# Rebuilding the backward pass of sliding-window attention: batching heads, folding a row sum into a matmul, and transposing by DMA

## The chip, the cores and the metric

The kernel runs on one core of one Trainium2 chip. The metric is the time of one execution on the device, in microseconds (us). "Span" is the time from the first to the last instruction in a profiled execution. The engines are PE (matmul), PEld (its weight loads), DVE (vector), ACT (activation), POOL (GpSimd) and SP (which only issues DMA here).

## The reference

Four layers run in the order A, B, A, B, and the kernel returns the output and the gradients of the inputs. A is linear attention, B is attention over a window of 256 keys. T = 2048 tokens, D = 640, 32 heads of 20 columns. The change concerns the backward pass of B.

```python
def _B_ref(x, wqkv, wo):
    H = 32; Dh = D // H; W = 256
    q, k, v = ...                                   # of x @ wqkv, per head
    scores = jnp.einsum("bhqd,bhkd->bhqk", q, k) * (Dh ** -0.5)
    mask = (idx[:, None] - idx[None, :] >= 0) & (idx[:, None] - idx[None, :] < W)
    p = _softmax(jnp.where(mask, scores, -1e9))
    o = jnp.einsum("bhqk,bhkd->bhqd", p, v)
    return o... @ wo
# x = x + A(ln(x)); x = x + B(ln(x)); x = x + A(ln(x)); x = x + B(ln(x)); then jax.vjp
```

With dP = dO Vᵀ and delta = the row sum of dO·o, the gradient of the scores is dS = p · (dP − delta). Then dV = pᵀ dO, dK = dSᵀ Q and dQ = dS K.

## The kernel before

Heads are padded to 32 columns, so that four heads make a group of 128 columns; there are 8 groups. Queries come in 16 blocks of 128; a block sees at most three key blocks, 384 keys. So a layer B has 128 units (group, block). The kernel keeps both P and dS with queries on the partitions. As they lie, they are the stationary operand of the matmuls of dV and dK; for dQ it is dS transposed (the run no_transpose, which gives dQ dS as it lies, has wrong numbers: relative error 0.137).

```python
for g in range(G):
    QTg, KTg, VTg, dOTg, qsl, ksl, dosl, osl = ...   # slabs of this group, loaded on the queues of SP and ACT
    dtmp, delta = ...                                # DVE: row sums of dO * o, for the group
    for b in range(TT):
        ...                                          # four score matmuls into s4
        for hh in range(4):
            nc.scalar.activation(p_sb[:, 0:cw], s4[:, hh, 0:cw], ACT.Exp, bias=nll[...], scale=self.c_att)
            self.apply_masks(p_sb, nkt)              # two affine_select of 128 columns on POOL
        for hh in range(4):
            nc.tensor.matmul(dp_ps[:, 0:cw], lhsT=dOTg[...], rhs=VTg[...], ...)
            nc.vector.scalar_tensor_tensor(out=ds_sb[:, 0:cw], in0=dp_ps[:, 0:cw], scalar=delta[:, b, hh:hh + 1],
                                           in1=p_sb[:, 0:cw], op0=ALU.subtract, op1=ALU.mult)
            self.transposes(dsT_ps, [ds_sb[:, i * P:(i + 1) * P] for i in range(nkt)])    # on PE
            nc.scalar.copy(dsT[:, 0:nkt, :], dsT_ps[:, 0:nkt, :])                         # ACT
            for i in range(nkt):
                nc.tensor.matmul(dqvk[:, hh, 2, 0:DH], lhsT=dsT[:, i, :], rhs=ksl[...], ...)   # dq
        ...                                          # dv and dk of block b-2, copies to dqkv
```

Each unit is written head by head, in order; p is normalised by a bias in the exponential (minus the log of the row sum).

The softmax here doesn't subtract the row's maximum and nothing guards it: scores larger than these inputs give would overflow.

## Time and profile before

The median before was 4579.31 us (three runs, 4574.68 to 4580.05). The two backward attention stages, from their first score matmul to the last copy into dqkv, take 714 and 712 us, together 31% of the span.

| stretch of the profile before | us |
|---|---|
| backward attention of layer 3 (1794.5 to 2508.3) | 713.8 |
| backward attention of layer 1 (3211.5 to 3923.9) | 712.4 |
| the dO projection ahead of each | 52.8 and 52.6 |
| whole span | 4575.2 |

These lines are from the profile page of the kernel before: the span, the busy time of each engine, and two of the rows by slices (each digit is one fortieth of the span, about 114 us, in tenths).

```profile
span 4575.2 us, 81842 instructions
...
PE 3399.5 (74%) x31053; PEld 1892.7 (41%) x31148; DVE 2278.5 (50%) x6268; ACT 1870.0 (41%) x3758; POOL 577.0 (13%) x1963
...
PEclk6969655696865568555555996799555555798688
DMA  7345411334541136112110124214421120123312
```

Slices 17 to 22 and 29 to 34 lie in the backward attention stages: the clock granted to PE is 0.5 there, and the DMA engines are mostly at a fifth of their time or less.

The table of windows shows the first of those stages: the length, then busy microseconds of each engine with the number of instructions, the granted clock, the DMA share and the bytes per microsecond (GB/s).

```profile
core 0: us, PE busy (x) PEld busy (x) DVE busy (x) ACT busy (x) POOL busy (x), PEclk, DMA share, GB/s
1794.00:2508.00 714.00, 607.18 (x6784) 293.58 (x6784) 344.59 (x656) 506.30 (x1280) 264.44 (x960) 0.50 0.18 45
```

No engine is full. PE has 607 of 714 us, but that includes 12 transposes a unit, and the DMA engines have 0.18.

The costliest groups of instructions of the page, within the changed stages: line, engine, operation, tiles, shapes and count; then busy us in all and mean ns of one; then idle time of the engine just before them and what ended it.

```profile
L827 DVE SCALAR_TENSOR_TENSOR ds_sb<-dp_ps,delta,p_sb 128x384 bf16<-128x384 f32 (+2 forms) x1024 | 582.4, 590 | 555.7 <-POOL p_sb L474 472.6
L834 ACT COPY dsT<-dsT_ps 128x384 bf16<-128x384 bf16 (+2 forms) x1024 | 472.6, 462 | 346.7 <-PE dsT_ps L155 310.4
L814 ACT ACTIVATE p_sb<-s_ps,nll 128x384 bf16<-128x384 f32 (+2 forms) x1024 | 557.7, 573 | 12.4 <-issue 6.8
L155 PE MATMUL dsT_ps<-ident,ds_sb 128*128 128x128 bf16 x2880 | 499.7, 295 | 51.5 <-ACT dsT L834 40.5
L471 POOL TENSOR_SCALAR_AFFINE_SELECT p_sb<-p_sb 128x128 bf16<-128x128 bf16 x1024 | 308.6, 303 | 1583.5 <-ACT p_sb L814 1532.8
```

The view of waits, over 2060 to 2400 us of the kernel before, says who waited for whom, in all, how often, and the longest:

```profile
POOL p_sb L471 <- ACT p_sb L814: 200.8, 174, 3.2
DVE ds_sb L827 <- POOL p_sb L474: 126.9, 110, 2.2
PEld L836 <- ACT dsT L834: 93.7, 132, 0.9
ACT dsT L834 <- PE dsT_ps L155: 76.8, 121, 2.8
```

There is no single culprit: masks wait for the exponential, dS for the mask, the copy of the transposes for PE, and dQ for the copy. It is one ring of short waits (at most 3.2 us).

### The profile page before, as it was taken

Reading aid. Unit: us, or ns where it says so; the run is one execution under the profiler, and the core shown is the slowest. Engines: PE = TensorE matmul, PEld = TensorE weight load, DVE = VectorE, ACT = ScalarE, POOL = GpSimd, SP = SyncE. Lnnn points to the kernel's source line nnn. Section 1 sums busy time; section 2 is a strip of 40 time slices with the busy share of each in tenths; the row PEclk is TensorE's granted clock in tenths of the full one; section 3 lists DMA queues with packets and bytes.
Section 4 is the critical chain, followed back from the end, with each engine's and each line's share of the span. In section 5 each row is a group of like instructions: output and inputs, shape, how many; then the busy total and the mean of one; then the engine's idle time right before and its main releaser. Section 6 shows DMA issues by size and latency. Waiting matters only on the chain. (4 is left out here: it accounts for less than half of the span.)

```text
span 4575.2 us, 81842 instructions
## 1 busy us (share of the span) xinstructions
PE 3399.5 (74%) x31053; PEld 1892.7 (41%) x31148; DVE 2278.5 (50%) x6268; ACT 1870.0 (41%) x3758; POOL 577.0 (13%) x1963
## 2 busy tenths in 40 slices
PE   3759666675866666888888884688688888876577
PEld 2334333433433343444443453355344444354335
DVE  4764455566435542445444365444444544265436
ACT  1413445341335523777776120113677777220202
POOL 2000000000000000333333000000333333000000
PEclk6969655696865568555555996799555555798688
DMA  7345411334541136112110124214421120123312
GB/s 280 126 162 178 127 43 29 122 128 149 171 137 29 43 104 157 37 37 72 34 34 24 67 78 157 74 62 119 107 48 37 50 52 2 61 77 123 138 62 73
DMA packets 507340, 412.69 MB, mean 90 GB/s; under 512 B 329024, under 2 KB 479040, under 8 KB 505024
## 3 DMA queue, kind: packets, MB, share of 16 engines
q1 hardware_dynamic: 242976, 201.95, 14.5%
q10 hardware_dynamic: 263968, 205.49, 14.5%
q8 instruction: 245, 4.01, 0.4%
q14 instruction: 151, 1.24, 0.1%
HBM read 232.72 MB, written 174.65 MB: 89 GB/s over the span
## 5 line engine op out<-in xcount | busy, mean ns | idle before, releaser
L827 DVE SCALAR_TENSOR_TENSOR ds_sb<-dp_ps,delta,p_sb 128x384 bf16<-128x384 f32 (+2 forms) x1024 | 582.4, 590 | 555.7 <-POOL p_sb L474 472.6
L834 ACT COPY dsT<-dsT_ps 128x384 bf16<-128x384 bf16 (+2 forms) x1024 | 472.6, 462 | 346.7 <-PE dsT_ps L155 310.4
L814 ACT ACTIVATE p_sb<-s_ps,nll 128x384 bf16<-128x384 f32 (+2 forms) x1024 | 557.7, 573 | 12.4 <-issue 6.8
L155 PE MATMUL dsT_ps<-ident,ds_sb 128*128 128x128 bf16 x2880 | 499.7, 295 | 51.5 <-ACT dsT L834 40.5
L471 POOL TENSOR_SCALAR_AFFINE_SELECT p_sb<-p_sb 128x128 bf16<-128x128 bf16 x1024 | 308.6, 303 | 1583.5 <-ACT p_sb L814 1532.8
L823 PE MATMUL dp_ps<-VTg,dOTg 32*128 32x384 bf16 (+2 forms) x1024 | 439.5, 470 | 24.6 <-DVE ds_sb L827 19.5
L433 PE MATMUL sT_ps<-QTg,KTg 32*128 32x128 bf16 x2880 | 254.4, 296 | 160.4 <-DVE o_t L448 116.8
L836 PEld LDWEIGHTS <-dsT 128*128 128x128 bf16 x2880 | 156.0, 108 | 461.5 <-ACT dsT L834 393.3
L836 PE MATMUL dqvk_ps<-ksl,dsT 128*128 128x20 bf16 x2880 | 214.1, 183 | 117.8 <-ACT dsT L834 111.3
L474 POOL TENSOR_SCALAR_AFFINE_SELECT p_sb<-p_sb 128x128 bf16<-128x128 bf16 x896 | 266.9, 298 | 0.0
L807 PE MATMUL s_ps<-KTg,QTg 32*128 32x384 bf16 (+2 forms) x1024 | 240.6, 477 | 33.5 <-ACT p_sb L814 13.2
L155 PEld LDWEIGHTS <-ds_sb 128*128 128x128 bf16 x2880 | 227.4, 116 | 80.3 <-issue 68.4
L547 PEld LDWEIGHTS <-dqT 128*128 128x128 bf16 x1920 | 185.5, 99 | 132.8 <-DVE dqT L541 31.8
L543 ACT COPY dqT<-dqT_ps 128x896 bf16<-128x896 bf16 x64 | 58.0, 906 | 398.4 <-PE dqT_ps L155 391.6
L396 PE MATMUL qkvp_ps<-WBpad,hnT 128*128 128x512 bf16 x928 | 217.1, 384 | 3.6 <-ACT hnT L239 1.6
L515 PEld LDWEIGHTS <-hn_bw 128*128 128x128 bf16 x1280 | 126.9, 99 | 199.6 <-issue 74.0
L855 PEld LDWEIGHTS <-p_sb 128*128 128x128 bf16 x2880 | 156.7, 106 | 78.5 <-issue 76.2
L433 PEld LDWEIGHTS <-KTg 32*128 32x128 bf16 x2880 | 101.5, 112 | 197.2 <-DVE o_t L448 141.9
L287 PE MATMUL qkv_ps<-WA,hnT 128*128 128x512 bf16 (+1 forms) x626 | 148.5, 373 | 46.1 <-ACT vv L295 17.5
L855 PE MATMUL dqvk_ps<-dosl,p_sb 128*128 128x20 bf16 x2880 | 179.4, 181 | 3.3 <-ACT dqkv L863 2.7
L855 PE MATMUL dqvk_ps<-qsl,ds_sb 128*128 128x20 bf16 x2880 | 173.4, 179 | 0.0
L547 PE MATMUL dh_ps<-WqTB,dqT 128*128 128x320 bf16 x960 | 138.6, 304 | 25.5 <-DVE dqT L541 11.1
(2490 smaller groups left out, 5872.5 us busy)
## 6 DMA issues: line engine op xcount, KB each, us to landing
qkvp_126<-qkvp_slab SPq DMA_DIRECT2D x16, 768.0 KB, 3.5
qkvp_130<-qkvp_slab ACTq DMA_DIRECT2D x16, 768.0 KB, 3.4
qkvT_127<-qkvT_slab ACTq DMA_DIRECT2D x32, 256.0 KB, 5.2
qkvT_131<-qkvT_slab SPq DMA_DIRECT2D x32, 256.0 KB, 4.1
KTg<-qkvT_127 SPq DMA_DIRECT2D x12, 512.0 KB, 3.6
QTg<-qkvT_127 ACTq DMA_DIRECT2D x12, 512.0 KB, 4.8
QTg<-qkvT_131 ACTq DMA_DIRECT2D x12, 512.0 KB, 4.9
KTg<-qkvT_131 SPq DMA_DIRECT2D x12, 512.0 KB, 3.6
```

Of the source, the lines that this page charges most:

```text
L155: self.nc.tensor.transpose(ps[:, i, :], s, self.ident)
L433: nc.tensor.matmul(sT[:, hh, i * P:(i + 1) * P], lhsT=KTg[HPAD * hh:HPAD * (hh + 1), kt * P:(kt + 1) * P], rhs=QTg[HPAD * hh:HPAD * (hh + ...
L471: nc.gpsimd.affine_select(out=e_sb[:, last:last + P], in_=e_sb[:, last:last + P], compare_op=ALU.is_ge, fill=0.0, base=0, pattern=[[-1, P] ...
L474: nc.gpsimd.affine_select(out=e_sb[:, 0:P], in_=e_sb[:, 0:P], compare_op=ALU.is_ge, fill=0.0, base=-1, pattern=[[1, P]], channel_multiplie ...
L547: nc.tensor.matmul(ps[:, ci, 0:cw], lhsT=dqT[:, k, :], rhs=WqT[:, k, ci * cw:(ci + 1) * cw], start=(k == 0), stop=(k == QTT - 1))
L807: nc.tensor.matmul(s4[:, hh, 0:cw], lhsT=QTg[HPAD * hh:HPAD * (hh + 1), b * P:(b + 1) * P], rhs=KTg[HPAD * hh:HPAD * (hh + 1), k0 * P:(k0 ...
L814: nc.scalar.activation(p_sb[:, 0:cw], s4[:, hh, 0:cw], ACT.Exp, bias=nll[:, b, hg:hg + 1], scale=self.c_att)
L823: nc.tensor.matmul(dp_ps[:, 0:cw], lhsT=dOTg[HPAD * hh:HPAD * (hh + 1), b * P:(b + 1) * P], rhs=VTg[HPAD * hh:HPAD * (hh + 1), k0 * P:(k0 ...
L827: nc.vector.scalar_tensor_tensor(out=ds_sb[:, 0:cw], in0=dp_ps[:, 0:cw], scalar=delta[:, b, hh:hh + 1], in1=p_sb[:, 0:cw], op0=ALU.subtrac ...
L834: nc.scalar.copy(dsT[:, 0:nkt, :], dsT_ps[:, 0:nkt, :])
L836: nc.tensor.matmul(dqvk[:, hh, 2, 0:DH], lhsT=dsT[:, i, :], rhs=ksl[:, k0 + i, HPAD * hh:HPAD * hh + DH], start=(i == 0), stop=(i == nkt - 1))
L855: nc.tensor.matmul(dvk_ps[:, hh, j, 0:DH], lhsT=src_tile[:, idx * P:(idx + 1) * P], rhs=rhs_sl[:, bb, HPAD * hh:HPAD * hh + DH], start=(i ...
```

## The change

The intent is to replace the chain of each head by larger steps, to take the transposes off PE and ACT, and to let four units overlap. In the new kernel:

- Exponentials and dS products take two heads (768 columns) per instruction, masks four heads (512 columns).
- The row sum is folded into dP: dO gets two more columns that hold −delta as a bfloat16 pair (high and low part), V gets ones there. dO is also multiplied by the inverse row sum, so the exponential needs no bias.
- One DMA transposes the whole dS of a unit (128 x 1536), issued on SP; it lands in SBUF and needs no copy.
- Step s does the scores of unit s, half of dS of s−1 and the other half of s−2, dV and dK of s−2, dQ of s−3.
- The seven slabs of the next group are loaded on POOL's DMA queue instead of the queues of SP and ACT.

The core of the diff, with cuts:

```diff
+    def ld(self, out, in_):
+            self.nc.gpsimd.dma_start(out=out, in_=in_)
...
+                        nc.vector.tensor_tensor(out=sl3[...], in0=ps..., in1=linv[...]..., op=ALU.mult)
+                    nc.vector.tensor_tensor(out=dtmp, in0=sl3[:, :, 0:DH], in1=o_t[...], op=ALU.mult)
+                    nc.vector.tensor_reduce(out=delta, in_=dtmp, axis=AX.X, op=ALU.add, negate=True)
+                    nc.vector.tensor_copy(sl3[:, :, DH], delta)
+                    nc.vector.tensor_sub(sl3[:, :, DH + 1], delta, sl3[:, :, DH])
...
-                        for hh in range(4):
-                            nc.scalar.activation(p_sb[:, 0:cw], s4[:, hh, 0:cw], ACT.Exp, bias=nll[:, b, hg:hg + 1], ...)
-                            self.apply_masks(p_sb, nkt)
-                            nc.vector.scalar_tensor_tensor(out=ds_sb[:, 0:cw], ..., op0=ALU.subtract, op1=ALU.mult)
-                            self.transposes(dsT_ps, [ds_sb[:, i * P:(i + 1) * P] for i in range(nkt)])
-                            nc.scalar.copy(dsT[:, 0:nkt, :], dsT_ps[:, 0:nkt, :])
+                nc.scalar.activation(ev[:, 2 * half:2 * half + 2], ps[:, :, 0:nkt * P]..., ACT.Exp, scale=c_att)
+                nc.vector.tensor_tensor(out=dv[:, hs], in0=ps[:, :, 0:nkt * P]..., in1=ev[:, hs], op=ALU.mult)
+                if half == 1:
+                    dsT_of[u] = pe.tile([P, 12, P], BF, name="dsT", bufs=4)
+                    nc.sync.dma_start_transpose(out=dsT_of[u][:, 0:4 * nkt, :], in_=ds_of[u][:, 0:4 * nkt * P])
...
+            for s in range(n + 3):
+                if s < n and units[s][1] == 4 and units[s][0] + 1 < G:
+                    load(units[s][0] + 1)
+                sa = scores(s, 0, "QT", "KT") if s < n else None
+                pb = scores(s - 2, 1, "dOT", "VT") if 0 <= s - 2 < n else None
+                ... expo(s, 0), dscore(s - 2, 1), scores(s, 1), scores(s - 1, 0), expo(s, 1), dscore(s - 1, 0)
+                ... dvk of s - 2
+                if 0 <= s - 3 < n:
+                    dq(s - 3, ps_o.tile([P, 3, 4, HPAD], F32, name="acc"))
```

## The prediction

> **What bounds it now.** By the table of windows, the two backward-attention stages run from 1794 to 2508 us and from about 3212 to 3924 us: 1426 of 4575 us, 5.6 us for each of 128 (group, block) units. No engine is full there: in the first, PE is busy 607 of 718 us, ACT 507, DVE 345, POOL 264, DMA share 0.19, granted clock 0.50. Each unit is a ring of waits (view of waits, 2060 to 2400 us): DVE's ds waits for POOL's mask (127 us), POOL for the exponential (201), ACT's dsT copy for the transposes (77), the dq weight loads for that copy (94). Back to back, a product costs 27 ns in the timeline (shown as 180).
>
> **Per full unit, durations from the trace.**
> - Removed: 12 PE transposes (295 ns each, three in 0.48), four dsT copies on ACT (4 x 482 ns = 1.93 us), four-way splitting of exp (4 x 594), ds (4 x 616) and masks (8 x 300 ns); dtmp/delta per group (2.97 us of DVE).
> - ACT after: two exps of 768 columns. An exp of 384 takes 594 ns, one of 1536 takes 1451, so about 0.80 us each; three copies of 0.24. Sum 2.3 us (was 5.0 with its copies).
> - DVE: two products of 768 columns; ds grows 1.05 ns a column from 616 ns at 384: about 1.0 us each.
> - POOL: two selects of 512 columns; 128 take 0.30 us, 640 take 0.94: 0.78 each, 1.6 us, plus building seven slab loads per group, unmeasured here.
> - PE: 36 products x 27 ns = 1.0 us, and eight score matmuls whose pairs overlap: about 2 us at clock 0.5.
> - DMA: one transpose of 384 KB per unit on the SP queue. [...] No transpose is in this trace; plain 512 KB loads land in 3.6 to 5.5 us.
>
> **Critical path.** ACT at 2.3 us a unit is the floor. In the built order dq follows its ds by about 1.3 steps. If a transpose takes 4 to 5 us from ds to landed, the step is held at 3 to 4 us by that latency. I take 3.5 us: 131 steps, 459 us, plus 15 us for the first loads, 474 against 713: 239 us saved per layer. The preceding dO stage is PE-paced at 2.6 us per tile and becomes DVE-paced: 2 x 0.69 + 0.82 + 0.77 + about 0.4 = 3.4 us, 12 us lost. Net about 225 x 2 = 450 us, with gentler group starts 480: **4100 us**, range 3880 to 4400. Faster by over 2%: 0.87; within 2%: 0.04; slower: 0.09.
>
> **What would show it.** Both stages at 400 to 560 us; granted clock still near 0.5; the largest PE wait in the stage is for the dsT DMA; ACT 60 to 75% busy; exp near 0.80 us, ds near 1.0, selects near 0.78; DMA share 0.5 to 0.8; dO stage 10 to 15 us longer; the rest unchanged.
>
> **What would make it wrong.** [...] issue on SP over 3 us each: then the stage is a DMA queue and at 5.5 us a transpose nothing is gained. POOL blocked by building load descriptors, delaying masks. If transposes land in under 3 us, steps near 2.6 us and about 3900 us.

131 steps of 3.5 us and 15 us are 474 us, 239 less than 713; less 12 for the dO stage that is about 225 a layer, 450 for both, 480 with the group starts, and 4575 − 480 is about 4100 us. The 4 to 5 us from ds to landed were the estimate; the trace before showed no transpose, only loads of 512 KB that landed in 3.6 to 5.5 us. The DMA share of 0.5 to 0.8 has no measured number behind it.

## The result

The changed kernel took 4141.86 us (median of four runs, 4127.17 to 4154.41), the kernel before 4578.9 us in the same series (four runs, 4574.68 to 4580.05). The ratio is 0.9045 with a 95% interval of 0.902 to 0.907. Ratios here are the mean time of one kernel's runs over that of the other's of the same rounds, so not quite the ratio of the medians. The change is 9.5% faster, inside the predicted range. The four runs of the changed kernel lie 27 us apart, and the profile below is of the slowest (4154.41), so its stages can be some 6 us each longer than in the median run; differences of that size between stages are not read below.

| stretch (profiled executions) | before | after | difference |
|---|---|---|---|
| backward attention, layer 3 | 713.8 | 486.8 | −227.0 |
| backward attention, layer 1 | 712.4 | 480.9 | −231.5 |
| dO projection, layers 3 and 1 | 105.4 | 121.2 | +15.8 |
| rest | 3043.6 | 3063.8 | +20.2 |
| span | 4575.2 | 4152.7 | −422.5 |

The profile page of the kernel after, the same lines, and the two DMA queues that matter (packets, bytes, share of 16 engines' span):

```profile
span 4152.7 us, 70886 instructions
...
PE 2862.4 (69%) x28268; PEld 1667.8 (40%) x28268; DVE 2122.0 (51%) x5628; ACT 1367.2 (33%) x2440; POOL 428.7 (10%) x651
...
PEclk6978855569687555865555898689955555997799
DMA  8345611043455110489998323311599897223221
...
q1 hardware_dynamic: 560304, 266.70, 28.4%
...
q0 software_dynamic: 16128, 58.73, 6.1%
```

The DMA row has new runs of 9, in the changed stages. Queue q1 carries SP's DMAs, with 560304 packets where it had 242976, because a transpose goes as packets of 256 bytes (368640 of them in the trace, 1536 for a full unit); q0 is POOL's new queue.

The table of windows for the first stage, with the columns as before:

```profile
1814.00:2301.00 487.00, 332.37 (x5344) 181.99 (x5343) 230.29 (x256) 259.01 (x639) 186.63 (x290) 0.50 0.92 157
```

PE lost its transposes (607 to 332 us), ACT its copies (506 to 259), and now no engine is busy for more than about 68% of the stage. The DMA share rose from 0.18 to 0.92.

The groups of instructions of the kernel after that answer to those before:

```profile
L866 DVE TENSOR_TENSOR ds<-sp,e 128x768 bf16<-128x768 f32 (+2 forms) x512 | 460.9, 907 | 516.7 <-PE sp L832 409.4
L847 ACT ACTIVATE e<-sp 128x768 bf16<-128x768 f32 (+2 forms) x512 | 392.1, 771 | 122.9 <-PE sp L832 100.6
...
L875 PE MATMUL acc<-ksl,dsT 128*128 128x20 bf16 x2880 | 124.8, 181 | 227.3 <-DMA dsT<-ds 226.9
...
L851 POOL TENSOR_SCALAR_AFFINE_SELECT e<-e 128x512 bf16<-128x512 bf16 x256 | 162.1, 633 | 570.0 <-issue 525.4
```

An exponential of 768 columns is 811 ns when the full shape is taken alone, a dS product 957 ns; the means above mix shapes. PE's last group names the new wait: products with the transposed dS wait for its DMA, 226.9 us in all, and their weight loads for another 312.

The view of waits from 2060 to 2300 us of the kernel after:

```profile
DVE ds L866 <- PE sp L832: 91.1, 86, 10.1
PEld L875 <- DMA dsT<-ds: 81.0, 44, 9.7
ACT dqkv L904 <- PE acc L875: 66.3, 30, 10.6
PE acc L875 <- DMA dsT<-ds: 58.6, 23, 9.3
```

Four entries of one chain: dS K waits for the transposed dS, the copy of its result waits for PE, and DVE's dS product waits for PE's scores, which stand behind it in PE's program. Waits of 10 us stand in a place where the longest was 3.2.

The view of the tile dsT (the transposed dS): the issue of its DMA on SP (min/median/max in ns), and the time from issue to landing.

```profile
L870 SPq DMA_TRANSPOSE dsT<-ds x256: 1189/1432/8839, 1819.9 to 3499.9; - x128
...
DMA to landing us min/median/max: 2.4/4.2/20.6
```

The median is 4.2 us, the longest 20.6. That spread is the finding, and the average of the stage hides it. From the start times of the transposes in the trace: in the last group of each layer, in which nothing is loaded, the 16 transposes start within 39.3 and 40.5 us, 2.6 to 2.7 us a unit. In groups during which the next slabs are loaded, 16 units take 54 to 73 us, and the longest step of each such group is 6 to 16.5 us. By the start times of the exponentials, the loss stands in blocks 1 to 6 of a group, where the loads are in flight: 3.6 to 7.7 us a step (mean of the seven groups), against 2.5 to 3.3 us in the blocks after them. The same view of waits inside a quiet stretch (2264 to 2298 us) has no long wait at all:

```profile
DVE ds L866 <- PE sp L832: 7.1, 19, 0.6
PEld L875 <- DMA dsT<-ds: 6.0, 11, 0.9
```

### The profile page after: what moved, and what is told of

It is laid out like the page before. It is cut to its first block, busy times and chain, and to the rows that moved or that the text cites. A ratio compares the mean times of both kernels' runs of the same rounds, so it can differ in the third digit from the quotient of the medians.

```text
span 4152.7 us, 70886 instructions
## 1 busy us (share of the span) xinstructions
PE 2862.4 (69%) x28268; PEld 1667.8 (40%) x28268; DVE 2122.0 (51%) x5628; ACT 1367.2 (33%) x2440; POOL 428.7 (10%) x651
## 3 DMA queue, kind: packets, MB, share of 16 engines
q1 hardware_dynamic: 560304, 266.70, 28.4%
## 5 line engine op out<-in xcount | busy, mean ns | idle before, releaser
L866 DVE TENSOR_TENSOR ds<-sp,e 128x768 bf16<-128x768 f32 (+2 forms) x512 | 460.9, 907 | 516.7 <-PE sp L832 409.4
L847 ACT ACTIVATE e<-sp 128x768 bf16<-128x768 f32 (+2 forms) x512 | 392.1, 771 | 122.9 <-PE sp L832 100.6
L832 PE MATMUL sp<-KT,QT 32*128 32x384 bf16 (+2 forms) x1024 | 284.7, 476 | 57.7 <-ACT e L847 32.6
L875 PE MATMUL acc<-ksl,dsT 128*128 128x20 bf16 x2880 | 124.8, 181 | 227.3 <-DMA dsT<-ds 226.9
L832 PE MATMUL sp<-VT,dOT 32*128 32x384 bf16 (+2 forms) x1024 | 246.4, 472 | 32.3 <-ACT e L847 21.1
L851 POOL TENSOR_SCALAR_AFFINE_SELECT e<-e 128x512 bf16<-128x512 bf16 x256 | 162.1, 633 | 570.0 <-issue 525.4
L551 PE MATMUL dh_ps<-WqTA,dqT 128*128 128x320 bf16 x960 | 140.4, 305 | 22.9 <-DVE dqT L545 10.3
L855 POOL TENSOR_SCALAR_AFFINE_SELECT e<-e 128x512 bf16<-128x512 bf16 x224 | 141.8, 633 | 0.0
L875 PEld LDWEIGHTS <-e 128*128 128x128 bf16 x2880 | 103.6, 106 | 94.7 <-issue 79.5
L875 PE MATMUL acc<-qsl,ds 128*128 128x20 bf16 x2880 | 134.0, 179 | 0.9 <-DVE ds L866 0.5
L875 PE MATMUL acc<-dosl,e 128*128 128x20 bf16 x2880 | 130.9, 181 | 4.7 <-ACT dqkv L904 4.6
```

The costliest lines, as they stand in the source:

```text
L551: nc.tensor.matmul(ps[:, ci, 0:cw], lhsT=dqT[:, k, :], rhs=WqT[:, k, ci * cw:(ci + 1) * cw], start=(k == 0), stop=(k == QTT - 1))
L832: nc.tensor.matmul(ps[:, j, 0:nkt * P], lhsT=slabs[g][ta][r0:r0 + HPAD, b * P:(b + 1) * P], rhs=slabs[g][tb][r0:r0 + HPAD, k0 * P:(k0 + nk ...
L847: nc.scalar.activation(ev[:, 2 * half:2 * half + 2], ps[:, :, 0:nkt * P].rearrange("p h (i k) -> p h i k", k=P), ACT.Exp, scale=c_att)
L851: nc.gpsimd.affine_select(out=ev[:, :, nkt - 1, :], in_=ev[:, :, nkt - 1, :], compare_op=ALU.is_ge, fill=0.0, base=0, pattern=[[0, 4], [-1 ...
L855: nc.gpsimd.affine_select(out=ev[:, :, 0, :], in_=ev[:, :, 0, :], compare_op=ALU.is_ge, fill=0.0, base=-1, pattern=[[0, 4], [1, P]], chann ...
L866: nc.vector.tensor_tensor(out=dv[:, hs], in0=ps[:, :, 0:nkt * P].rearrange("p h (i k) -> p h i k", k=P), in1=ev[:, hs], op=ALU.mult)
```

## The experiments

Theories:

- **T, throughput.** The DMA engines are busy 0.92 of the stage and set its length through the time that transposes take.
- **C, collision.** The stage is long because transposes meet the slab loads on the DMA engines. Form Q of it, an assumption: the engines alternate between queues packet by packet, so a transposing packet of 256 bytes waits for one of 4096 bytes each time.
- **L, latency.** Every transpose takes 4 us or more from issue to landing, and dQ follows too closely (the mechanism of the prediction).
- **P, POOL.** Issuing the loads on POOL (0.53 to 1.20 us each in the kernel after; that POOL builds descriptors in that time is the record's reading, which no trace shows) holds the masks up.

These names sort the theories as they stood at the end; the expectations on record tell in their own words what each theory was when its run was sent.

Stage lengths below are of the profiled executions, layer 3 / layer 1, and both layers agree to 3%. Experiments without an interval were run once each; the runs of the kernel before beside them took 4568 to 4573 us. All edits are to the kernel after. The clock granted was 0.50 in both stages of every run, from their first to their last microsecond.

| run | edit | numbers | stage us | total us |
|---|---|---|---|---|
| after | | right | 486.8 / 480.9 | 4141.86 |
| loads_once | slabs of group 0 for all groups | wrong | 363.8 / 366.8 | 3915.30 |
| no_transpose | dS used untransposed | wrong | 350.3 / 349.1 | 3880.44 |
| neither | both | wrong | 336.7 / 335.4 | 3849.80 |
| loads_act | loads on ACT's queue | right | 447.3 / 448.5 | 4075.21 |
| lag6 | dQ six units later | right | 415.6 / 407.7 | 4004.24 |
| spread | one load per unit | right | 457.0 / 445.8 | 4086.57 |
| loads_sp | loads on SP's queue | right | 414.5 / 417.1 | 4008.13 |
| pe_transpose | transposes on PE again | right | 541.0 / 540.6 | 4259.88 |
| lag6_sp | lag6 and loads_sp | right | 371.8 / 370.8 | 3925.67 |
| lag6_act | lag6 and loads_act | right | 401.2 / 401.4 | 3984.89 |
| no_pipeline | a unit from start to end | right | 550.9 / 544.8 | 4276.18 |
| small_packets | loads_act, all rows cut to 256 bytes | right | 460.0 / 458.6 | 4107.48 |

### Loads, transposes, and both taken away

```diff
 # loads_once
+            for g_ in range(1, G):
+                slabs[g_] = slabs[0]
-                if s < n and units[s][1] == 4 and units[s][0] + 1 < G:
-                    load(units[s][0] + 1)
 # no_transpose
-                    dsT_of[u] = pe.tile([P, 12, P], BF, name="dsT", bufs=4)
-                    nc.sync.dma_start_transpose(out=..., in_=...)
-                dsT = dsT_of.pop(u)
+                dsT = ds_of[u].rearrange("p (c k) -> p c k", k=P)
 # neither: both edits
```

> Only group 0's slabs are loaded and all eight groups use them (wrong result on purpose). Theory D (the 16 DMA engines are shared by the transposes and the slab loads, and the loads make the transposes land late): every group runs like the last one of the changed kernel, which has no loads beside it, about 2.5 us a step; each attention stage 325 to 345 us instead of 481 to 487, total near 3850 us, no transpose landing above 6 us. Rival F (a fixed landing latency of the transposes sets the step): stages stay within 20 us of 484. This run alone does not tell D from rival P (building the load descriptors holds POOL and so the masks).

> No transposes: dq takes ds itself as its stationary operand (wrong result on purpose); the loads stay. Theory D: nothing in the ring waits for a DMA any more, and the loads alone (about 12 us of all engines per group) hide; stages 310 to 345 us at 2.35 to 2.6 us a step, total near 3830. If the loads hurt by another way than through the transposes (rival P), the stages stay well over 400 us.

> Neither transposes nor repeated loads (wrong result on purpose): the engines' own floor. If the clean step of 2.5 us is set by DMA time of a transpose (2.3 us of all 16 engines), the step falls to about 2.35 us, ACT's sum; if it is set by the ring of ACT, PE and DVE, it stays at 2.5. Stages 305 to 335 us, total near 3820.

Measured, as means of both layers: with neither 336 us; the transposes alone add 29 (365), the loads alone add 14 (350), and both together add 148 (484). So 105 us of a layer (148 − 29 − 14) exist only when both are there; given the spread of the changed kernel's runs, this is good to about 10 us. That speaks for C, and against L and P: with loads_once the transposes still go to landing in 3.8 us at the median, as this line of the dsT tile view shows, yet the stage is 365 us.

```profile
DMA to landing us min/median/max: 2.4/3.8/7.6
```

The run with neither gives the floor that the engines set. Its window, with the columns as before:

```profile
1808.00:2144.00 336.00, 318.99 (x5340) 188.81 (x5337) 230.71 (x256) 249.27 (x639) 146.90 (x241) 0.50 0.04 9
```

336 us over 131 steps are 2.56 us each, with PE busy 319 of 336 us (95%) at the clock 0.50. The ends of matmuls are modelled in these profiles, so the busy time alone does not name the bottleneck; the waits agree with it. Over the stage PE and its weight loads wait 15 us in all for other engines and DMAs, while DVE and ACT wait for PE, as these lines of the view of waits of neither, 1900 to 2050 us, show:

```profile
DVE ds L866 <- PE sp L832: 21.5, 62, 0.7
ACT dqkv L893 <- PE acc L874: 19.5, 47, 0.8
```

A quiet step of the kernel after is close to this floor. In the last group of a layer, first to last unit, the exponentials take 40.6 and 41.3 us there, and 38.7 us in neither: transposes that land in 3.9 us (median of the quiet stretch) cost a step 0.1 to 0.2 us.

### Loads on ACT's queue

```diff
-            self.nc.gpsimd.dma_start(out=out, in_=in_)
+            self.nc.scalar.dma_start(out=out, in_=in_)
```

> The slab loads are issued from the ACT queue instead of POOL. Theory D: the same bytes go through the same 16 engines, so the stages stay at 470 to 510 us and the total within 2% of 4142 us, perhaps a little longer because ACT issues. Rival P (POOL blocked by descriptor building): POOL is free, stages drop to 340 to 380 us, total 3850 to 3930.

The stage fell to 448 us, by 36 of the 148, between the two expectations (470 to 510, and 340 to 380). P cannot be the main cause: with POOL still issuing every load, but no transposes, the stage is 350. What remained at 448 became clear only with the last experiment.

### dQ later, loads spread, loads on the transposes' own queue

```diff
 # lag6
-            for s in range(n + 3):
-                if s < n and units[s][1] == 4 and units[s][0] + 1 < G:
+            for s in range(n + 6):
+                if s < n and units[s][1] == 7 and units[s][0] + 1 < G:
-                if 0 <= s - 3 < n:
-                    dq(s - 3, ...)
+                if 0 <= s - 6 < n:
+                    dq(s - 6, ...)          # and 7 buffers of dsT instead of 4
 # spread: load(g + 1) is cut into its seven loads, one each at blocks 4 to 10; a one-element POOL
 # copy from e of that unit into the slab holds each load back until then
 # loads_sp
-            self.nc.gpsimd.dma_start(out=out, in_=in_)
+            self.nc.sync.dma_start(out=out, in_=in_)
```

> dq runs three steps later (six behind the scores instead of three, seven dsT buffers, next group's loads placed at block 7), so that the in-order PE queue need not wait for a late transpose; the DMA work is the same. If the cost of the loads is landing latency that PE sits out (theory L, bursts), the stages fall from 484 to 390 to 410 us, which is the DMA work (120 full transposes x 2.35 us + 7 groups of loads x 12.4 us = 369) at about 0.93; total near 3970. If it is the throughput of the DMA engines alone (theory T), they are already 92% busy and the stages stay above 460.

> The seven slab loads of the next group are held back so that one starts in each of the steps of blocks 4 to 10 (a one-element copy that reads that step's e stands before each), instead of starting as soon as the old slab is free. Theory L (bursts): backlog is spread, transposes land in under 9 us, stages 400 to 430 us, total near 4000. Theory T: the same work, stages 465 to 490 us.

> The slab loads go through the SP queue, the same as the transposes[...]. If the alternation of two queues is what slows the transposes beyond the sum of the work, the stages come near those with loads on ACT or lower (430 to 450 us); if an SP load delays the next transposes by its whole length, a few transposes land late by 5 to 12 us and the stages are 450 to 490.

That PE takes its work in order, as lag6 supposes, shows in the kernel after: from its last product at about 3038.1 us PE does nothing for 13.85 us, until the transposed dS lands at 3051.86; the scores that the program puts behind dQ, and that DVE waits for (14.19 us), start only at 3052.23. The sum of 369 us in lag6's expectation is an estimate. A full transpose of 1536 packets of 24.4 ns (mean of the quiet stretch), over 16 engines, is 2.34 us; in no_transpose the DMA share was 0.30 over 280 us, 84 us for about seven groups of loads, 12 us each.

With lag6 the same transposes and the same loads went through in 412 us, so T falls: the engines had not been at a limit of throughput at 484. Transposes landed even later, as the line of the dsT tile of lag6 shows, but six units of slack took most of that up.

```profile
DMA to landing us min/median/max: 2.4/5.8/23.5
```

Spreading the loads brought only 33 us: 451 us a stage, between the two expectations (400 to 430, and 465 to 490), and the longest landing was 16.3 us, not under 9. Giving them to the queue that carries the transposes brought 68 (416 us), and the longest landing fell from 20.6 to 8.3 us:

```profile
DMA to landing us min/median/max: 2.4/4.3/8.3
```

On one queue, loads of 4096-byte packets and loads of 256-byte packets came in turns longer than a packet: on SP's queue in both stages of the kernel before, 170 microseconds have starts of such packets, and 7 of them have both sorts (on ACT's queue 3 of 222). Loads and transposes on one queue were not counted so. On two queues, both sorts did move in the same microsecond: in 315 of 904 in the stages of the kernel after. One stretch of the kernel after, by counts of packets in its trace; from 3040 to 3046 us two transposes and three to five loads are in flight:

```
us of the trace   4096-byte packets, POOL's queue   256-byte packets, transposes' queue
3040 to 3042             96 (218 ns mean)                  104 (34 ns mean)
3042 to 3044            128 (235 ns mean)                  141 (30 ns mean)
3044 to 3046            108 (277 ns mean)                  120 (36 ns mean)
3052 to 3054              0                                966 (20 ns mean)
3056 to 3058              0                               1285 (21 ns mean)
```

Here the two queues moved about as many packets each, though one sort is sixteen times the size of the other; a transpose issued at 3031.23 landed at 3051.86. When the loads were through, transposes moved 8 to 10 times as many packets in the same time (two stretches shown). Form Q would have about one for one, and the counts of this stretch would agree with that. But the stretch is not typical. Cut both stages into stretches of 2 us. In 94 of them at least 60 load packets start, and at every moment some transpose has been issued for 2 us or more and has not landed. Only 13 of the 94 show between 0.8 and 1.25 transposing packets for one of a load; the middle half runs from 0.9 to 6.7. So the collision is shown, by the runs that take one side away; form Q, that it goes packet by packet, is not.

### Both cures together

The edits of lag6 and of loads_sp, or of lag6 and of loads_act, in one kernel.

> Both remedies together: dq three steps later and the loads on the SP queue. If they take away different parts of the loss (waiting for late landings; transposes alternating with the loads' packets), the stages approach the sum of the DMA work, 369 us at 95% busy, so 385 to 400 us, total 3930 to 3970, ratio to the kernel before 0.86 to 0.87. If they take away the same part, the stages stay at 407 to 417 us, ratio 0.876.

> dq three steps later with the loads on the ACT queue. Loads on ACT alone gave 448 us a stage, the lag alone 412. If what ACT's issue saved was only lateness, the lag already covers it: 400 to 415 us, ratio 0.873 to 0.878. If issue on ACT now delays the exponentials, over 415.

lag6_sp took 3925.67 us (four runs, 3924.77 to 3929.01), ratio to before 0.8592 (0.8578 to 0.8607), with right numbers: it beats both kernels. Its stage is 371 us, 113 of the 148 us recovered. The gains of the two edits were 72 and 68 when made alone, so they overlap only in part. lag6_act took 3984.89 us, ratio 0.8726 (0.8713 to 0.8739), and its stage of 401 us is in the range expected. The first stage of lag6_sp in the table of windows, and the landing of its transposes:

```profile
1809.00:2181.00 372.00, 334.36 (x5344) 187.02 (x5343) 229.35 (x256) 252.92 (x640) 146.92 (x240) 0.50 1.14 205
```

```profile
DMA to landing us min/median/max: 2.5/4.8/8.0
```

Here the DMA share is 1.14 and 205 GB/s are moved, where it was 0.92 and 157 GB/s in the longer stage. So a DMA share of 0.92 was not saturation: the share passed 1 here, so the times of packets that it adds up overlap. The transposes take longer at the median (4.8 us) than in the kernel after (4.2), and the stage is 113 us shorter.

### The transposes back on PE, and no pipelining by hand

```diff
 # pe_transpose
-                    nc.sync.dma_start_transpose(out=..., in_=...)
+                for half in range(2):
+                    ... six nc.tensor.transpose into PSUM, then nc.vector.tensor_copy to dsT
 # and one accumulator buffer instead of two
 # no_pipeline: the loop body does scores, expo, dscore, dvk and dq of unit s one after the other
```

> This part undone alone: dS is transposed on PE again (12 transposes per step, copies of 768 columns by DVE), everything else as changed; [...] the accumulator has one buffer instead of two. PE gets 12 x 0.107 us more at clock 0.5 on a floor of 2.56 us a step, DVE 1.1 us more: about 3.9 us a step, stages about 510 us, total near 4190; so the DMA transpose would be worth 25 us a layer in spite of its contention. Below 470 us the DMA transpose is a loss.

> The software pipeline of the changed kernel undone alone: each step does its own unit from scores to dq; transposes by DMA, loads on POOL as changed. A transpose lands in 3.7 us without loads, and a chain of scores, exp, mask, dP, ds, landing, dq is about 0.5 + 1.6 + 1.3 + 0.5 + 1.9 + 3.7 + 0.5 = 10 us, of which the build's own reordering hides some: 6 to 8 us a step, stages 750 to 1000 us, total 4700 to 5200, slower than the kernel before. If the reordering of the build already hides the latency, the stages stay under 550 us and the pipeline written by hand was not needed.

The first expectation: its 0.107 us is the step between starts of successive transposes of dS on PE in the kernel before (106 or 107 ns in 724 pairs; 60 ns in 917 others). The 3.7 us of the second one compare with landings of 3.75 and 3.87 us (medians of the last groups of the kernel after).

With transposes on PE the stage is 541 us: before's 713 to 541 is the work of batching, the fold and the pipeline together (172 us a layer; batching and the fold were not undone one by one), and the DMA transpose is worth 57 more as the change uses it, or 170 as lag6_sp uses it. This comparison has a flaw: the single accumulator is part of it. Its view of waits, 2060 to 2300 us, has this line near the top, DVE's copy waiting for PE's transposes:

```profile
DVE dsT L910 <- PE dsT_ps L907: 68.8, 95, 1.4
```

Without the hand-made pipeline the stage is 548 us, 64 more than in the kernel after, not the 750 and more that was expected; it is just under the mark of 550 set for "not needed", but the hand-made order is still worth these 64. The build's scheduler orders instructions itself and recovers a good part of the overlap: in this run's trace, PE in places does dQ of one unit between the two dP halves of a later one, which the program does not say. So the experiment undoes less than its edit says.

### Loads in small packets

```diff
 # on top of loads_act, for QT, KT, VT and dOT
-                    r[n] = psl.tile([P, T], BF, name=n)
-                    self.ld(r[n], sv["qkvT"][...])
+                    r[n] = psl.tile([P, TT, P + 16], BF, name=n)
+                    self.ld(r[n][:, :, 0:P], sv["qkvT"][...].rearrange("p (t k) -> p t k", k=P))
```

> The run with the loads on ACT's queue, with one thing more: the four feature-major slabs (QT, KT, VT, dOT) are loaded into a tile with 16 columns of padding after each 128, so that each of their rows of 4096 bytes goes as 16 packets of 256 bytes, as the rows of the other three slabs already do. Same bytes, same queues, same places in the program; 14336 packets a group instead of 6656. Alternation packet by packet (Q): while loads are in flight a transpose's packet now waits behind one packet of some 20 to 40 ns instead of one of 160 to 236 ns, so the longest landing falls from 11.2 us to under 7.5 us and the stage, 448 us with the loads on ACT, falls to 405 to 435. Rival (timing): what made the stalls with the loads on ACT is only when and how many bytes are asked for at once, so 2.1 times as many packets for the same bytes make the loads slower (an estimate: 14336 packets of about 20 ns over 16 engines are 18 us a group, where there were 4 times 1.3 and 3 times 2.6 us, 13 us): the longest landing stays at 10 us or more and the stage is 445 to 490 us. Numbers are correct in both.

Its counts of packets are from the shapes; in the kernel before, loads with rows of 256 bytes did go as 256-byte packets on ACT's queue (26624 from 1820 to 2505 us).

Half of each expectation came true. The longest landing fell from 11.2 us with loads_act to 7.5, and landings of over 7.5 us from 20 of 256 to none, as alternation by packets wants it; but the loads' issues are spread differently too (ksl's takes 3.0 us at the median, where it took 5.5), so this does not prove it. These are the landing lines of the dsT tile, loads_act first, small_packets second:

```profile
DMA to landing us min/median/max: 2.4/4.0/11.2
```

```profile
DMA to landing us min/median/max: 2.4/4.0/7.5
```

But the stage is 459 us (4107.48 us in all, four runs, 4100.85 to 4109.68; ratio 0.8995, 0.898 to 0.901), not the 405 to 435 of Q; loads_act had 448. So with the loads on ACT something else than the landing sets the length. ACT's timeline of small_packets shows it (start in us, length in us, engine, line, operation; ACTq is ACT's own sequencer issuing a DMA):

```profile
3179.28 1.66 ACT L847 ACTIVATE e<-sp 128x768 bf16<-128x768 f32 x2
3180.13 0.53 ACTq L143 DMA_DIRECT2D VT<-qkvT  x1
3180.70 1.35 ACTq L143 DMA_DIRECT2D dOT<-dOpT  x1
...
3182.09 3.45 ACTq L143 DMA_DIRECT2D qsl<-qkvp  x1
3185.58 3.41 ACTq L143 DMA_DIRECT2D ksl<-qkvp  x1
3189.09 3.33 ACTq L143 DMA_DIRECT2D dosl<-dOpt  x1
3192.53 1.51 ACT L847 ACTIVATE e<-sp 128x768 bf16<-128x768 f32 x2 [11.47 <-DMA qsl<-qkvp]
```

For 11.5 us ACT runs no exponential, because its sequencer is issuing three DMAs of 3.4 us each, and two short ones ahead of them. (The releaser named, a DMA, is the last one by the profile; the issues fill the gap without a hole.) loads_act has the same stall; the issues of one of its slabs, against those of the same slab on POOL in the kernel after, in two fences (min/median/max ns of an issue):

```profile
L143 ACTq DMA_DIRECT2D ksl<-qkvp x16: 2694/5504/9045, 1806.6 to 3327.4; - x16
```

```profile
L143 POOL DMA_DIRECT2D ksl<-qkvp_130 x8: 1161/1179/1188, 1812.8 to 2200.6; - x8
```

So loads_act exchanged one cost for another: shorter landings for an ACT that stands still once in each group. Its size can be read from the start times of the exponentials: their units start 2.67 us apart in undisturbed stretches of all these runs. What units lost by starting more than 3.5 us apart sums to 95 us a layer in loads_act, and 75 of these are the one longest pause of each of the seven groups with loads (11.5 to 15.8 us). In small_packets it is 69 of 106, in lag6_act 50 of 51: slack for dQ removes every other pause, and this one stays. Neither theory had priced it. On SP the issues of that slab are slow as well (3.5 us at the median in loads_sp), but SP has nothing to do there except issue. lag6_act (401) is 30 us longer than lag6_sp (371); by the same count only 10 of these lie in pauses of over 3.5 us (51 against 41), so this pause is not the whole of that difference.

### What stays open

POOL's slab loads all show as 4096-byte packets in the kernel after (14336, 128 a load), even those with rows of 256 bytes, while on the queues of SP and ACT such loads show as 256-byte packets in the kernel before (38912 from 1820 to 2505 us). Moving the loads to another queue also moves their issue in time, because the build lets a load wait only for its buffer (in loads_sp SP's issues of loads waited for PE's scores, 18.8 us in 13 waits from 1900 to 2100 us). So the 68 us of loads_sp are not split between "one queue", "other packets" and "other moments". lag6 likewise moves the place of the loads in the program, from block 4 to block 7, along with dQ. small_packets supports alternation by packets through its landings only, since its length is set elsewhere. The last 35 us between lag6_sp (371) and neither (336) were not chased, nor were the 20 us by which the rest of the program grew.

## Why the prediction was right or wrong

**Right: the size.** 4100 us was predicted and 4141.86 measured; the stage was 474 predicted and 484 measured (mean). Step durations were read well: exp 0.80 predicted and 0.81 measured, dS 1.0 and 0.96. The clock stayed at 0.50, the largest PE wait in the stage is for the dsT DMA, and the copies and PE transposes are gone.

**Wrong: the mechanism of the step.** The prediction said "the step is held at 3 to 4 us by that latency. I take 3.5 us". The average fits, but no step looks like it. Quiet steps take 2.6 to 2.7 us although transposes land in 3.9 us, and steps during slab loads take up to 16.5. The missing term was the collision of transposes with the loads: 105 us a layer, against 29 for the transposes alone. The alternative offered, "If transposes land in under 3 us, steps near 2.6 us and about 3900 us", names the state without collision nearly to the number (loads_once, 3915 us), but with the wrong condition. That the total came out is partly luck: a steady cost was assumed where a bursty one was, of the same size.

**Wrong: the floor.** "ACT at 2.3 us a unit is the floor" — it is PE at the clock 0.50, which the prediction had put at "about 2 us": 2.56 us a step, with PE 95% busy and hardly waiting in the run with neither. ACT was busy 259 of 487 us, 53%, not the 60 to 75% predicted.

**Wrong: the DMA figures.** The share was 0.92, not 0.5 to 0.8. Measured, 157 GB/s were moved in all in the stage, 205 in lag6_sp, and no transpose of a full unit (384 KB) landed in under 3.6 us in any run; the landings of 2.4 us are of shorter units at the start of a group. The forecast thought of the rate as a constant; landings were very late only beside the loads (up to 20.6 us, against 7.6 in loads_once).

**Wrong, small.** POOL's selects took 0.63 us, not 0.78. The dO projection lost 7 and 9 us, not 12. "Gentler group starts" were to bring 30 us; the first blocks of a group are the very place where the time was lost. And the rest of the program grew by 20 us.

## What to carry to other kernels

When a stage has two DMA streams, price them together: a latency-bound stream of small packets beside a bulk stream of large ones can wait far longer than it needs alone (landings of up to 20.6 us here, against 7.6), and the average step does not show it, while the maximum of issue-to-landing does. The cures are slack between producer and consumer (three more units were worth 72 us of 148) and, for the bulk stream, the queue of the small one, on an engine that only issues (68 us here); issues of several microseconds kept ACT from its exponentials for 11.5 us here. To find such an interaction, take each stream away alone and then both, wrong numbers allowed: 29, 14 and 148 us say at once that neither is dear by itself.

## Further measurements

- The same seven loads gave a stage of 484 us on POOL's queue, 448 on ACT's and 416 on SP's, beside transposes on SP. Queue, packet sizes and moments of issue change together in these runs, so they do not show which of them does it. Transposes landed in up to 20.6 us beside the loads of the kernel after, and in up to 7.6 without repeated loads.
- In loads_act the load of ksl, a slab with rows of 256 bytes, held ACT's sequencer 5.5 us at the median (2.7 to 9.0) of the 12.1 us to its landing; POOL needed 1.2 us for it in the kernel after. It is not so for every such slab: qsl, issued just before, took 0.4 us, and dosl 3.2.
- The DMA share was 1.14 in lag6_sp, at 205 GB/s.
- The run with neither had PE busy 319 of 336 us (as the profile models it), and a granted clock of 0.50 throughout: a busy PE did not raise it there.
- 256-byte packets take 18 ns at the median (24 in the mean) in transposes in a quiet stretch of the kernel after, and 18 ns (19 in the mean) in the plain slab loads of the kernel before. A unit of 384 KB went as 1536 packets of 256 bytes, a load of 512 KB with long rows as packets of 4096 bytes at 159 ns (median, kernel before), so that per byte the packets of the transpose took 1.8 times as long (18/256 against 159/4096).
